# An expert layer's Strassen products: a list scheduler written in the kernel, sums kept in DRAM, and three products split once more

## The chip, the cores and the metric

The kernel runs on one core of one Trainium2 chip. The metric is the device time of one execution, in microseconds, as the median of several runs. Lower is better.

## The reference

Block-sparse attention (4 batches, 8 heads, 768 positions, head size 64) is followed by a mixture of 8 experts over its output `x` (3072 tokens of 512 features):

```
logits = x @ w_gate
P = exp(logits - logits.max())
for _ in range(8):
    P /= P.sum(1, keepdims=True) + 1e-09
    P /= P.sum(0, keepdims=True) + 1e-09
    P *= N / E
for e in range(8):
    h = maximum(x @ w1[e], 0)        # w1[e]: 512 x 1024
    out += P[:, e:e+1] * (h @ w2[e]) # w2[e]: 1024 x 512
```

Every expert sees every token, so the expert part is 8 times two large matrix products.

## The kernel before, in words

The attention comes first, in an order that is written out by hand: every step has a place in a table of time steps, and `in_order` chains the instructions of each engine to one another in that order. It leaves `x`, transposed, in DRAM (`xd`), for each batch as the seven operands that a Strassen-like scheme (Winograd's form) needs. Every operand is kept as two float16 halves, a high and a low one, so one product of float32 quality is three float16 matmuls: high by high, high by low, low by high.

The expert part runs 32 passes, `i = 4 e + b` for expert `e` and batch `b` (768 tokens). A pass has two stages:

- Stage one (`stage1`, L1199 on) computes `h` transposed: 1024 hidden features by 768 tokens, split in two by two quarters, so seven products instead of eight. Each product is 512 features by 384 tokens with 256 inner features and is made in four strips (`qi`) of 128 features. One strip of one product is one PSUM bank and 6 matmuls of 384 columns (2 chunks of 128 inner features, 3 float16 terms; L1208). DVE and ACT take each bank out at once: `comb` (L1220) adds it to what the earlier products gave. Then ReLU (ACT, in place), four sums or differences on GpSimd, and for each of the seven results a high half (ACT, L1230) and a low half (DVE L1234 or L1240, GpSimd L1240). These are the seven `h` operands of stage two.
- Stage two (`stage2`, L1333) makes seven products, each 384 tokens by 256 output features with 512 inner ones, in three strips (`ci`) of 128 tokens: one strip is one bank and 12 matmuls of 256 columns. The products 0, 5, 6 share a bank in turn (`FOLLOWS`), and 4, 2 another. DVE adds each bank, times the expert's weight of each token, to the sum of the outputs `acc` in SBUF (L1357; ACT writes the first ones, L1354).

All of `acc` (4 batches) stays in SBUF from the first expert to the last. PSUM has four banks for stage one (`ps_h`) and four for stage two (`ps_y`), each handed out in turn. The loop at the end interleaves strips of stage one of pass `i + 1` with products of stage two of pass `i`. The side work (reads, low halves, weight sums and splits, the balance iterations of P) is put into slots by `Slots`, which counts the planned load of each engine; the final order on each engine is then chosen by the framework's own scheduler, so an instruction of the expert part can also stand ahead of the attention's last ones.

The weights of one expert, 2 MB each for `w1` and `w2`, share one raw buffer. For each matrix ACT makes eight magnitude sums (L108), PE spreads their maximum over the partitions (L114), GpSimd forms the sums of quarters (L1087, L1094 for `h`), ACT and DVE split each of the seven operands (L1072, L1076). The `x` operands are loaded anew for each pass (L227, 7 x 384 KB).

Of the kernel before, what the change touches and what calls it, by code (L numbers as in the profile page):

```python
# [24 lines left out]
TOP = 2.0 ** 12  # L25
# [4 lines left out]
HDOWN = 2.0 ** -20  # L30
HUP = 2.0 ** 20
EPS = 1e-9
PORDER = (0, 1, 5, 6, 3, 4, 2)
NHT = 30
NU = 8
LOP = (2, 3)
LOPE = (2, 3, 5)
NLE = 99
LEADS, LAGS = (1.0, 1.0, 1.0), (1.0, 1.0, 1.0)
SD = (2, 3, 4, 5)  # L40
PRE, LB2, LB1 = 0, 1, 1
PIN = 0
TW = 100
TF = 146
HQ = 300
NHA = 10
LATE = 40
# [3 lines left out]
LAV = 3  # L51


@with_exitstack
def tile_sparse_attention_moe(
# [79 lines left out]
    def scale_power(tag, s, inv):  # L135
# [6 lines left out]
        nc.vector.tensor_scalar(s, s, TOP, None, ALU.mult)  # L142
        nc.vector.tensor_scalar(inv, a, 1.0 / TOP, None, ALU.mult)

# [35 lines left out]
    def scale_steps(which, e, vector=nc.vector, scalar=nc.scalar):  # L180
# [18 lines left out]
        def power():  # L199
            vector.tensor_reduce(out=a, in_=wr["all", which], axis=AX.X, op=ALU.max)  # L200
            vector.tensor_scalar(a, a, TINY, HUGE, ALU.max, ALU.min)
            ai = a.bitcast(I32)
            vector.tensor_scalar(ai, ai, 0x7F800000, None, ALU.bitwise_and)
            vector.reciprocal(s, a)
            vector.tensor_scalar(s, s, TOP, None, ALU.mult)
            vector.tensor_scalar(inv, a, 1.0 / TOP, None, ALU.mult)

# [138 lines left out]
    def finish_x(b):  # L346
        xf = xfs.pop(b).rearrange("p k c t -> p k (c t)")
        quad = {
            (j, k): xf[:, j * KH : (j + 1) * KH, k * TH : (k + 1) * TH]
            for j in range(2) for k in range(2)  # L350
        }

        def split(src, p, nm):
            st = xst.tile([P, 2, KH, TH], F16, tag="xs", name=f"xs_{b}_{nm}")
            nc.scalar.activation(st[:, 0], src, AF.Copy)
            nc.vector.tensor_tensor(out=st[:, 1], in0=src, in1=st[:, 0], op=ALU.subtract)
            if p is not None:
                nc.sync.dma_start(out=xd[b][:, p], in_=st)
            return st

        def plain(k):
            sts = [
                split(quad[j, k], {(0, 0): 0, (1, 0): 1, (1, 1): 2}.get((j, k)), f"b{j}{k}")
                for j in range(2)
            ]
            ps = bank[0](f"lg_{b}_{k}")
            for i in range(CH):
                for kc in range(KD):
                    for m, (l, w) in enumerate(((1, gh), (0, gl), (0, gh))):
                        nc.tensor.matmul(  # L370
                            ps[:, i * NE : (i + 1) * NE],
                            lhsT=sts[kc // KH][:, l, kc % KH, i * P : (i + 1) * P],
                            rhs=w[:, kc],
                            start=(kc == 0 and m == 0), stop=(kc == KD - 1 and m == 2),
                        )
            t0 = b * NC + k * CH
            nc.vector.tensor_scalar(
                lg[:, t0 : t0 + CH].rearrange("p t e -> p (t e)"), ps[:, : CH * NE],
                inv_v[:, b : b + 1], inv_g, ALU.mult, ALU.mult,
            )  # L380

        def diff(nm, x, y, out, p):
            nc.gpsimd.tensor_tensor(out=out, in0=x, in1=y, op=ALU.subtract)
            split(out, p, nm)

        x00, x01, x10, x11 = (quad[j, k] for j in range(2) for k in range(2))
        return [
            lambda: plain(0),
            lambda: plain(1),
            lambda: diff("t1", x01, x00, x00, 4),  # L390
            lambda: diff("t3", x11, x01, x01, 6),
            lambda: diff("t2", x11, x00, x00, 5),
            lambda: diff("t4", x10, x00, x10, 3),
        ]

    with ExitStack() as actx:
# [18 lines left out]
        plan = xfp.tile([P, 2, S], BF16, tag="xf", name="plan")  # L415
        onehot = plan[:, 0]
# [148 lines left out]
        def scale_v(b):  # L565
            sv[b] = small.tile([P, 1], F32, tag="sv", name=f"sv_{b}")
            scale_power(f"v{b}", sv[b], inv_v[:, b : b + 1])
# [246 lines left out]
        def split_gate():  # L814
            scale_power("g", sg, inv_g)
# [116 lines left out]
        xlast = finish_x(B - 1)  # L932

    class InOrder:
        def __init__(self, engine):
            self.engine = engine

        def __getattr__(self, name):
            call = getattr(self.engine, name)
            if not PIN:  # L940
                return call
            return lambda *a, **kw: tc.keep_in_program_order(call(*a, **kw))

    class Pinned:
        vector, scalar, gpsimd = (InOrder(x) for x in (nc.vector, nc.scalar, nc.gpsimd))
# [3 lines left out]
    )  # L949
    sk = mpool("sk", 1)  # L950
    upool = mpool("upool", NU)
    hA = mpool("hA", 1)
    hB = mpool("hB", 1)
    big = mpool("big", 1)
    def spare(n):
        return sk.tile([P, n], F32, name=f"spare_{next(count)}")

    count = iter(range(99))
    ps_h = mpool("ps_h", 4, space=PSUM)
    ps_y = mpool("ps_y", 4, space=PSUM)  # L960

    DH = DM // 2
    w2p = [big.tile([P, 2, KF // 2, DH], F16, name=f"w2p_{p}") for p in range(NP)]
    hfree = [
        (hA if n < NHA else hB).tile([P, 2, TH], F16, name=f"h_{n}") for n in range(NHT)
    ]
    accs = {b: big.tile([P, NC, DM], F32, name=f"acc_{b}") for b in range(B // 2)}
    bank[0] = lambda nm: ps_y.tile([P, 512], F32, tag="py", name=nm)
    spread_bank[0] = lambda nm: ps_h.tile([P, 512], F32, tag="ph", name=nm)

    def acc(t):
        return accs[t // NC][:, t % NC]

    def finish_late():
        slots.need(("late", 0, 0))
        late.close()
        right = mpool("right", 1, side="right")
        for b in range(B // 2, B):
            accs[b] = right.tile([P, NC, DM], F32, name=f"acc_{b}")

    aside = set()

    def not_earlier(fn):
        made = nc.cur_bb.bb.instructions
        n = len(made)
        fn()
        for ins in list(made[n:]):
            if ins.engine not in SIDE:
                continue
            for old in reversed(made[:n]):  # L990
                if old.engine == ins.engine and old.name not in aside:
                    tc.add_manual_dep(ins, old.name, behind, reason="not_ahead_of_its_place")
                    break
            aside.add(ins.name)

    class Slots:
        def __init__(self):
            self.now, self.pe, self.busy = 0, 0.0, [0.0, 0.0, 0.0]
            self.urgent, self.lazy = [], []
            self.last = 0  # L1000

        def add(self, fn, key, delay=1, lazy=False, dve=0.0, act=0.0, pool=0.0, gap=0):
            queue = self.lazy if lazy else self.urgent
            queue.append((fn, key, self.now + delay, (dve, act, pool), gap))

        def charge(self, costs):
            self.busy = [x + c for x, c in zip(self.busy, costs)]

        def run(self, queue, n):
            fn, key, _, costs, _ = queue.pop(n)  # L1010
            self.charge(costs)
            if queue is self.lazy:
                self.last = self.now
            if key[0] in ("scale", "w1", "w2"):
                not_earlier(fn)
            else:
                fn()

        def fits(self, costs):
            return all(  # L1020
                not c or x <= self.pe + lead
                for x, c, lead in zip(self.busy, costs, LEADS)
            )

        def tick(self, pe, dve, act=0.0):
            self.now += 1
            self.pe += pe
            self.busy = [max(x, self.pe - lag) for x, lag in zip(self.busy, LAGS)]
            self.charge((dve, act, 0.0))
            n, held = 0, set()  # L1030
            while n < len(self.urgent):
                _, key, ready, costs, _ = self.urgent[n]
                if key not in held and ready <= self.now and self.fits(costs):
                    self.run(self.urgent, n)
                    n, held = 0, set()
                    continue
                held.add(key)
                if key[0][0] == "sum":
# [358 lines left out]
    for i in range(NI):  # L1397
# [35 lines left out]
        if last:  # L1433
            parts[1]()
# [43 lines left out]
```

## Time and profile before

| what | value |
|---|---|
| median of 3 runs | 2236.8 us (2235.66 to 2239.47) |
| span of the profiled execution | 2232.8 us |
| PE busy | 2162.7 us (97%) |
| weight loads busy | 1596.3 us (71%) |
| DVE, POOL, ACT busy | 1671.7, 1412.6, 1285.1 us |
| first stage-one matmul | 414.07 us |
| DMA | 192.36 MB, 86 GB/s |

The page gives no time of the profiled execution other than its span; the time beside it is the median of the runs. PE is TensorE's matmuls, PEld its weight loads, DVE VectorE, ACT ScalarE, POOL GpSimd, SP the engine that issues most DMAs. Matmuls overlap, so the mean duration of one (as in a group's row) is longer than the distance at which they start. A wait is shown in square brackets, with the instruction that ended it.

### The profile page before, as it was taken

What the parts mean: (1) busy time and instruction counts of PE and PEld (TensorE: products, weight loads), DVE (VectorE), ACT (ScalarE), POOL (GpSimd) and SP (SyncE); (2) the same over time, 40 slices, a digit from 0 to 9 for tenths busy, and PEclk for the clock granted to TensorE, in tenths of its full rate; (3) what the DMA queues carried; (4) which work ended last, traced back from release to release, by engine and by line L of the source; (5) the groups of instructions that cost most, each with busy time, mean ns of one, the idle gap of its engine ahead of it and who ended that gap; (6) DMA issues with size and microseconds to landing.
All of it is one profiled execution on the core that took longest, in us unless ns stands there. A gap on an engine that the chain in (4) does not pass through costs nothing.

```text
span 2232.8 us, 47313 instructions
## 1 busy us (share of the span) xinstructions
PE 2162.7 (97%) x18892; PEld 1596.3 (71%) x18892; DVE 1671.7 (75%) x2927; ACT 1285.1 (58%) x2393; POOL 1412.6 (63%) x1481
## 2 busy tenths in 40 slices
PE   6999999889999999999999999999999999999999
PEld 4777766566777777777777777777677767776777
DVE  8888888778778767866786678667866786678664
ACT  5788888754566546554555455545554555455442
POOL 5556678685568555855685658565856585658553
PEclk9999999999999999999999999999999999999999
DMA  7766965312121212121212121212121212121221
GB/s 167 151 154 138 209 146 126 130 69 88 51 88 50 88 50 88 50 89 50 88 50 88 50 88 50 89 50 88 50 88 50 88 51 88 51 88 58 79 79 51
DMA packets 195347, 192.36 MB, mean 86 GB/s; under 512 B 132125, under 2 KB 150581, under 8 KB 195125
## 3 DMA queue, kind: packets, MB, share of 16 engines
q1 hardware_dynamic: 194560, 189.30, 29.3%
q8 instruction: 148, 2.42, 0.5%
q14 instruction: 75, 0.61, 0.1%
q10 hardware_dynamic: 564, 0.03, 0.0%
HBM read 140.54 MB, written 17.30 MB: 71 GB/s over the span
## 4 chain that ended last, share of the span: by engine, by line
PE 64%; DVE 11%; POOL 9%; ACT 7%; issue 4%; DMA 4%; DVEq 0%; SPq 0%; POOLq 0%; ACTq 0%
PE py L1333 26%; PE p L1208 25%; PE u L767 3%; DMA r<-in_moe_w_dram 3%; PE m L669 2%; PE m L672 2%; PE t L702 2%; PE t L705 2%; ACT h L1230 2%; POOL r L1087 2%; ACT unread L108 2%; POOL s L1282 2%; POOL h L1240 1%; DVE attic L1076 1%; POOL r L1094 1%
## 5 line engine op out<-in xcount | busy, mean ns | idle before, releaser
L1333 PE MATMUL py<-w2p,h 128*128 128x256 f16 x8064 | 952.4, 273 | 12.2 <-ACT acc L1354 4.2
L1333 PEld LDWEIGHTS <-h 128*128 128x128 f16 x8064 | 787.7, 98 | 154.0 <-issue 16.6
L1240 POOL TENSOR_TENSOR h<-u,h 128x384 f16<-128x384 f32 x128 | 124.4, 972 | 558.8 <-ACT h L1230 541.4
L1208 PEld LDWEIGHTS <-attic 128*128 128x128 f16 x3072 | 299.5, 98 | 202.2 <-issue 20.5
L1208 PE MATMUL p<-attic 128*128 128x384 f16 x2304 | 412.0, 326 | 12.7 <-DVE a L1220 8.0
L1208 PE MATMUL p<-arena 128*128 128x384 f16 x2304 | 415.3, 326 | 5.9 <-DVE u L1220 2.7
L1357 DVE SCALAR_TENSOR_TENSOR acc<-py,spare,acc 128x256 f32<-128x256 f32 (+1 forms) x588 | 295.0, 514 | 145.3 <-PE py L1333 143.2
L1208 PEld LDWEIGHTS <-arena 128*128 128x128 f16 x2304 | 225.2, 98 | 134.1 <-issue 7.8
L1230 ACT ACTIVATE h<-c 128x384 f16<-128x384 f32 x256 | 132.5, 520 | 319.9 <-DVE c L1220 263.0
L1220 DVE SCALAR_TENSOR_TENSOR a<-p,a 128x384 f32<-128x384 f32 x384 | 211.2, 550 | 22.7 <-PE p L1208 16.6
L678 DVE TENSOR_REDUCE top<-m 128x1 f32<-128x768 f32 x192 | 181.7, 951 | 46.7 <-PE m L672 45.8
L710 ACT ACTIVATE pe<-t,qk 128x768 int32<-128x768 f32 x192 | 172.3, 899 | 68.7 <-PE t L705 60.3
L1230 ACT ACTIVATE h<-s 128x384 f16<-128x384 f32 x128 | 66.8, 522 | 174.3 <-POOL s L1282 174.2
L1230 ACT ACTIVATE h<-r 128x384 f16<-128x384 f32 x256 | 131.3, 519 | 61.3 <-POOL r L1094 58.3
L1240 DVE TENSOR_TENSOR h<-s,h 128x384 f16<-128x384 f32 x128 | 106.2, 830 | 79.5 <-ACT h L1230 79.3
L1094 POOL TENSOR_TENSOR r<-s,r 128x384 f32<-128x384 f32 x128 | 153.6, 1200 | 10.0
L1094 POOL TENSOR_TENSOR c<-c,r 128x384 f32<-128x384 f32 x128 | 151.1, 1180 | 10.0
L1282 POOL TENSOR_TENSOR s<-a,u 128x384 f32<-128x384 f32 x128 | 140.9, 1101 | 17.3 <-ACT a L1279 17.1
L1208 PE MATMUL p<-arena,attic 128*128 128x384 f16 x768 | 146.2, 326 | 5.4 <-ACT a L1255 4.7
L1240 POOL TENSOR_TENSOR h<-r,h 128x384 f16<-128x384 f32 x128 | 133.9, 1046 | 18.3 <-ACT h L1230 15.2
L724 POOL TENSOR_SCALAR pl<-pe 128x768 f16<-128x768 uint16 x112 | 96.3, 864 | 70.9 <-ACT pe L710 68.8
L1087 POOL TENSOR_TENSOR r<-r 128x256 f32<-128x256 f32 (+1 forms) x106 | 119.0, 1148 | 31.0 <-DVE arena L1076 31.0
(206 smaller groups left out, 3717.3 us busy)
## 6 DMA issues: line engine op xcount, KB each, us to landing
arena<-xd SPq DMA_DIRECT2D x128, 384.0 KB, 3.9
attic<-xd SPq DMA_DIRECT2D x96, 384.0 KB, 4.2
r<-in_moe_w_dram SPq DMA_DIRECT2D x16, 2048.0 KB, 8.7
arena<-in_q_dram SPq DMA_DIRECT2D x16, 384.0 KB, 4.3
arena<-in_k_dram SPq DMA_DIRECT2D x16, 384.0 KB, 4.7
arena<-in_v_dram SPq DMA_DIRECT2D x4, 1536.0 KB, 7.8
xd<-xs_t SPq DMA_DIRECT2D x16, 384.0 KB, 2.9
out_dram<-acc SPq DMA_DIRECT2D x48, 128.0 KB, 1.7
```

The costliest lines, as they stand in the source:

```text
L678: nc.vector.tensor_reduce(out=tops[n][:, c : c + 1], in_=sc[:, :S], axis=AX.X, op=ALU.max)
L710: nc.scalar.activation(pe, sc[:, :S], AF.Exp, bias=EXP_SHIFT, scale=qk[n // 2][3])
L724: nc.gpsimd.tensor_scalar(lo, low, FINE, 1.0, ALU.mult, ALU.mult)
L1087: lambda c=c: Pinned.gpsimd.tensor_tensor(out=out[:, c], in0=x[:, c], in1=y[:, c], op=op),
L1094: nc.gpsimd.tensor_tensor(out=out, in0=x, in1=y, op=ALU.subtract)
L1208: nc.tensor.matmul(ps, lhsT=w1p[p][:, l, kc, fs], rhs=xp[p][:, r, kc], start=(kc == 0 and m == 0), stop=(kc == KH - 1 and m == 2),)
L1220: nc.vector.scalar_tensor_tensor(out=t, in0=ps, scalar=HDOWN, in1=other, op0=ALU.mult, op1=ALU.add)
L1230: nc.scalar.activation(h[:, 0], src, AF.Relu if relu else AF.Copy)
L1240: eng.tensor_tensor(out=h[:, 1], in0=src, in1=h[:, 0], op=ALU.subtract)
L1282: nc.gpsimd.tensor_tensor(out=s1, in0=a1, in1=u3, op=ALU.add)
L1333: nc.tensor.matmul(py, lhsT=hs[i, p, kc][:, l, tsl], rhs=w2p[p][:, r, kc], start=(old is None and kc == 0 and m == 0), stop=(kc == KF // 2 ...
L1357: nc.vector.scalar_tensor_tensor(out=dst, in0=src, scalar=c, in1=dst, op0=ALU.mult, op1=ALU.add)
```

## The change

The attention is unchanged, but for scale constants (`TOP1`, `HDOWN`, `HUP`). The expert part is written anew:

- Every step is a job with its engine or a choice of two (DVE or GpSimd), a planned duration, the jobs that it needs, and the buffers that it takes and drops. `Plan.run` is a list scheduler: it runs through planned time and starts on each engine, among the jobs that are ready, the one with the earliest deadline; on PE the one with the earliest planned place `pt`. Stage one and stage two are two streams with an order of their own. The order found is the program's: `in_order` chains all of it, on each engine, behind the attention's last instruction.
- In stage one a bank X takes the products 0, 5, 4, 2 one after another, without being cleared; after each the sum is read. So PE waits for a read before it goes on in the bank.
- From expert 1 on the products 6, 3 and 1 (`TWO`) of stage one are themselves made of seven products of quarters, for all strips at once: 21 groups of 6 matmuls of 192 columns instead of 12 groups of 6 of 384. Their operands are sums of quarters: of `w1` in SBUF (`sums`, on GpSimd for each expert, then split by ACT and DVE), of `x` prepared once in the first four passes (`prep_x`) and kept in DRAM (`xsd`), from where `xs` is loaded in each pass.
- `acc` is no longer kept in SBUF. Each pass loads two pieces of 768 KB, adds, and stores them (`accd`, in DRAM); three tiles are handed round.
- The output is stored in pieces of 384 KB.

The core of it:

```diff
-        a1 = fresh("a1")
-        nc.scalar.activation(a1, product(0), AF.Copy, scale=HDOWN)
-        tick(0, 1)
-        r11 = fresh("r11")
-        comb(r11, product(1), a1)
...
+    def run(self):
...
+                    if e == "PE":
+                        best = min(ok, key=lambda j: (j.pt is not None, j.pt if j.pt is not None else j.seq))
+                    else:
+                        for j in sorted(ok, key=lambda j: (j.dl, j.seq)):
...
+        def inner_group(p, r, bk, fresh):
...
+            def fn():
+                for c in range(2):
+                    for m, (l, rr) in enumerate(((0, 0), (0, 1), (1, 0))):
+                        nc.tensor.matmul(
+                            bk.tile[:, c * HT : (c + 1) * HT], lhsT=lhs(l, c), rhs=rhs(rr),
+                            start=(fresh and c == 0 and m == 0), stop=(m == 2),
+                            skip_group_check=True,
+                        )
...
+        def inner_product(p, addend=None):
...
+            j0, e0 = go(0, X, True, deps)
+            ta, ca = spot(X, 0, 0, j0, e0)
+            j1, e1 = go(1, Z, True, ())
...
+            j6, e6 = go(6, Y, True, ())
+            tc_, cc = spot(Y, 1, 1, j6, e6)
+            j5, e5 = go(5, X, False, (ca,))
+            tb, cb = spot(X, 1, 0, j5, e5)
+            j3, e3 = go(3, Y, False, (cc,))
...
+            j4, e4 = go(4, X, False, (cb,))
...
+            j2, e2 = go(2, X, False, (wrote[1, 1],))
...
+        if two:
+            got[6] = inner_product(6)
+            got[3] = inner_product(3, got[6])
+            got[1] = inner_product(1)
...
+            if two:
+                for q, (j, end) in outer(0, X, True, {}).items():
+                    r_[q] = scaled_add(cell(R, q), bank(X[q]), cell(R, q), [j] + rdep, dl=end + SLK)
+                for q, (j, end) in outer(5, X, False, {q: (r_[q],) for q in qis}).items():
+                    c_[q] = scaled_add(cell(C, q), bank(X[q]), cell(C, q), [j] + cdep, dl=end + SLK)
+                for q, (j, end) in outer(4, X, False, {q: (c_[q],) for q in qis}).items():
+                    u_[q] = scaled_add(cell(U, q), bank(X[q]), cell(U, q), [j] + udep, dl=end + SLK)
...
+                for q, (j, end) in outer(0, X, True, {}).items():
+                    k0[q] = scaled_copy(cell(R, q), bank(X[q]), (j,), take=first(R, q), dl=end + SLK)
+                for q, (j, end) in outer(1, Z, True, {}).items():
+                    r_[q] = scaled_add(cell(R, q), bank(Z[q]), cell(R, q), (j, k0[q]), drop=(Z[q],), dl=end + SLK)
...
+        pieces = [hold("acc") for _ in range(2)]
+        loaded = {}
+        if e:
+            for j in range(2):
+                ld = plan.dma(
+                    lambda j=j: nc.sync.dma_start(out=pieces[j].tile, in_=accd[b][j]), 768,
+                    (accstore[i - B, j],), take=(pieces[j],),
+                )
...
+        if e < NE - 1:
+            for j in range(2):
+                accstore[i, j] = plan.dma(
+                    lambda j=j: nc.sync.dma_start(out=accd[b][j], in_=pieces[j].tile), 768,
+                    tuple(writes[j]), drop=(pieces[j],),
+                )
...
+    S1A = NP * NF * 0.978
+    S1B = len(TWO) * 7 * 0.497 + (NP - len(TWO)) * NF * 0.978
+    S2 = NP * CH * 1.312
...
+        stage2(i, clock + SHIFT, length)
...
+            stage1(i + 1, clock, length)
+        clock += length
+    plan.run()
+    for fn in plan.order():
+        in_order(fn)
```

## Rows read from the trace of the kernel before

**Rows 1.** The page's busy line: us, share of the span, instructions.

```profile
PE 2162.7 (97%) x18892; PEld 1596.3 (71%) x18892; DVE 1671.7 (75%) x2927; ACT 1285.1 (58%) x2393; POOL 1412.6 (63%) x1481
```

**Rows 2.** Busy time by stretch: length, then engines, granted clock, DMA share, GB/s.

```profile
414.00:500.00 86.00, 75.16 (x535) 50.43 (x532) 66.42 (x106) 55.45 (x117) 63.28 (x60) 1.00 0.19 66
500.00:650.00 150.00, 144.18 (x1162) 107.48 (x1161) 118.98 (x233) 80.09 (x166) 87.41 (x80) 1.00 0.22 77
700.00:2229.00 1529.00, 1507.04 (x11521) 1124.99 (x11518) 1105.07 (x1959) 792.73 (x1593) 957.35 (x907) 1.00 0.20 69
```

**Rows 3.** Groups by line and form, PE: busy us, mean ns, idle before.

```profile
L1333 PE MATMUL py<-w2p,h 128*128 128x256 f16 x8064 | 952.4, 273 | 12.2 <-ACT acc L1354 4.2 <-DVE acc L1357 3.5 <-ACT w2p L1072 1.4
L1208 PE MATMUL p<-arena 128*128 128x384 f16 x2304 | 415.3, 326 | 5.9 <-DVE u L1220 2.7 <-DVE a L1220 1.8 <-DVE c L1220 0.9
```

**Rows 4.** Timeline of PE, undisturbed groups: start, length, instructions merged.

```profile
609.97 3.09 PE L1208 MATMUL p<-arena 128*128 128x384 f16 x18
612.90 1.14 PE L1208 MATMUL p<-arena,attic 128*128 128x384 f16 x6
...
621.05 2.78 PE L1333 MATMUL py<-w2p,h 128*128 128x256 f16 x24
623.67 0.33 PE L1208 MATMUL p<-arena 128*128 128x384 f16 x1
```

**Rows 5.** Timeline of PE, first and last of 45 short matmuls.

```profile
412.72 0.19 PE L767 MATMUL u<-vq,pl 128*128 128x66 f16 x1
...
414.04 0.19 PE L767 MATMUL u<-vh,pe 128*128 128x66 f16 x1
```

**Rows 6.** Groups by line and form, weight loads of those matmuls.

```profile
L767 PEld LDWEIGHTS <-pe 128*128 128x128 f16 x2304 | 118.4, 97 | 5.9 <-issue 0.8
```

**Rows 7.** Timeline of PE, ACT, DVE, where the attention ends.

```profile
414.07 3.09 PE L1208 MATMUL p<-arena 128*128 128x384 f16 x18
...
424.97 0.27 PE L114 MATMUL u<-ident,ma_w 128*128 128x128 f32 x1
...
433.69 0.49 PE L798 MATMUL u<-ident,xn 128*128 128x128 f32 x3
...
416.93 0.63 ACT L108 ACTIVATE unread<-r 128x512 bf16<-128x512 f32 x1 [3.06 <-DMA r<-in_moe_w_dram]
...
423.86 0.15 DVE L194 TENSOR_REDUCE ma_w<-mx_w 128x1 f32<-128x8 f32 x1
```

**Rows 8.** Groups by line and form, side engines.

```profile
L1220 DVE SCALAR_TENSOR_TENSOR a<-p,a 128x384 f32<-128x384 f32 x384 | 211.2, 550 | 22.7 <-PE p L1208 16.6
L1255 ACT ACTIVATE a<-p 128x384 f32<-128x384 f32 x128 | 61.4, 480 | 45.1 <-PE p L1208 44.2
L1279 ACT ACTIVATE a<-a 128x384 f32<-128x384 f32 x128 | 66.3, 518 | 3.5 <-DVE a L1220 2.6
L1087 POOL TENSOR_TENSOR r<-r 128x256 f32<-128x256 f32 x64 | 62.4, 1002 | 0.0
L1072 ACT ACTIVATE w2p<-r,sw 128x1024 f16<-128x1024 f32 x48 | 54.4, 1136 | 15.2 <-POOL r L1087 15.2
L1076 DVE SCALAR_TENSOR_TENSOR w2p<-r,sw,w2p 128x1024 f16<-128x1024 f32 x48 | 66.1, 1378 | 12.9 <-ACT w2p L1072 12.9
```

**Rows 9.** Timeline of DVE and PE, a wait of PE for an add.

```profile
1386.48 0.54 DVE L1220 SCALAR_TENSOR_TENSOR a<-p,a 128x384 f32<-128x384 f32 x1
...
1387.08 1.14 PE L1208 MATMUL p<-attic 128*128 128x384 f16 x6 [1.34 <-DVE a L1220]
```

**Rows 10.** The page's DMA issues: count, KB each, median us to landing.

```profile
attic<-xd SPq DMA_DIRECT2D x96, 384.0 KB, 4.2
r<-in_moe_w_dram SPq DMA_DIRECT2D x16, 2048.0 KB, 8.7
...
out_dram<-acc SPq DMA_DIRECT2D x48, 128.0 KB, 1.7
xd<-xs_b SPq DMA_DIRECT2D x12, 384.0 KB, 3.0
```

More of the change, by code (lines that the diff above doesn't have):

```diff
@@ L344, in plan_x @@
             at(T + 3, FIRST, x_store, b, nm, p)
[L346 to L394, printed above, removed]
     with ExitStack() as actx:
@@ L931, in tile_sparse_attention_moe @@
                 in_order(fn, *a)
[L932 to L945, printed above, removed]
     mpool = lambda name, bufs, **kw: ctx.enter_context(
@@ L981, in tile_sparse_attention_moe @@
[L981 to L1038, printed above, removed]
-                    held.update((("h", key[1], p),) + key[1:] for p in (2, 4, 5, 6))
-                n += 1
-            while self.lazy and self.due(self.lazy[0]):
-                self.run(self.lazy, 0)
-        def due(self, item):
-            _, _, ready, costs, gap = item
-            return max(ready, self.last + gap) <= self.now and self.fits(costs)
-        def settle(self, i, qi):
-            while any(x[1][1:] <= (i, qi) for x in self.urgent):
-                self.run(self.urgent, 0)
-        def need(self, key):
-            for queue in (self.urgent, self.lazy):
-                while any(x[1] == key or x[1][0] == key for x in queue):
-                    self.run(queue, 0)
@@ L1057, in tile_sparse_attention_moe @@
-    ET = mybir.EngineType
-    SIDE = (ET.DVE, ET.Activation, ET.Pool, ET.PE)
-    slots = Slots()
-    def scale_w(which, e):
-        parts, whole, spread, power = scale_steps(which, e, Pinned.vector, Pinned.scalar)
-        key = ("scale", which, e)
-        for k, part in enumerate(parts):
-            slots.add(part, key, 8 if k == 0 else 1, True, act=0.65)
-        slots.add(whole, key, 1, True, dve=0.1)
-        slots.add(spread, key, 1, True, gap=5)
-        slots.add(power, key, 1, True, dve=0.8, gap=2)
@@ new lines, in tile_sparse_attention_moe, with v3, seq @@
+    accd = [
+        [dram.tile([P, CH, DM], F32, name=f"accd_{b}_{j}") for j in range(2)] for b in range(B)
+    ]
+    xsd = [dram.tile([P, NP, 2, 4, TH // 2], F16, name=f"xsd_{b}") for b in range(B)]
+    sums = {}
+    shelf["xs"] = [xst.tile([P, 2, KH, TH], F16, tag="xs", name=f"stage_{n}") for n in range(4)]
+    plan = Plan(shelf)
+    job, hold = plan.job, plan.hold
+    def v3(t):
+        return t.rearrange("p (c t) -> p c t", c=2)
+    def seq(steps, deps=(), **kw):
+        last = tuple(deps)
+        for eng, dur, fn in steps:
+            last = (job({eng: dur}, fn, last, **kw),)
+        return last[0]
@@ L1139, in first, with split @@
[L1139 to L1143 removed]
+        stored = {}
+        def split(src, p, deps):
+            st = hold("xs")
+            hi = job({"ACT": 0.83}, lambda: nc.scalar.activation(st.tile[:, 0], src, AF.Copy), deps, take=(st,))
+            lo = job(
+                {"DVE": 1.3},
+                lambda: nc.vector.tensor_tensor(out=st.tile[:, 1], in0=src, in1=st.tile[:, 0], op=ALU.subtract),
+                (hi,),
+            )
+            if p is not None:
+                stored[p] = plan.dma(
+                    lambda: nc.sync.dma_start(out=xd[b][:, p], in_=st.tile), 384, (lo,), drop=(st,)
+                )
+            return st, lo
@@ new lines, in tile_sparse_attention_moe, with raw_load, scale_jobs, make @@
+    scaled, split_done, used1, used2 = {}, {}, {}, {}
+    last_s3 = [()]
+    raw_free = [()]
+    pwe = {}
+    def raw_load(which, e):
+        return plan.dma(lambda: load_w(which, e), 2048, raw_free[0])
+    def scale_jobs(which, e, loaded):
+        cell = {}
+        def make():
+            cell["steps"] = scale_steps(which, e)
+        parts = []
+        last = job({"-": 0.0}, make, (loaded,))
+        for k in range(8):
+            last = job({"ACT": 0.81}, lambda k=k: cell["steps"][0][k](), (last,))
+            parts.append(last)
+        whole = job({"DVE": 0.16}, lambda: cell["steps"][1](), parts)
+        bk = hold("s1", ordered=False)
+        def spread():
+            spread_bank[0] = lambda nm: bk.tile
+            cell["steps"][2]()
+        pe = job({"PE": 0.3}, spread, (whole,), take=(bk,))
+        power = job({"DVE": 1.2}, lambda: cell["steps"][3](), (pe,), drop=(bk,), rush=True)
+        scaled[which, e] = power
+        return parts, power
```

1228 lines of the change are left out of this document (873 added, 355 removed).

## The prediction

> **What bounds the kernel now.** I read the page's busy line first: TensorE (PE) is busy 2162.7 of 2232.8 us, 97%, far above DVE, POOL and ACT [rows 1]. That is an average, so the second view is the busy time by stretch. Of the 1529 us from 700 to 2229 us PE is busy 1507.0, so 22.0 are idle (1.4%), with DVE at 72%, POOL at 63% and ACT at 52%; the expert part's start is worse: 10.8 us idle of 86 (414 to 500 us) and 5.8 of 150 (500 to 650 us) [rows 2]. The clock is granted in full throughout. So in the expert part, which is four fifths of the span, the time is the number of columns that PE streams, plus some 39 us of gaps.
>
> The third view gives the price of a column. Busy means overlap (273 and 326 ns a matmul [rows 3]), so I take the distance of starts: eighteen 384-column matmuls run from 609.97 to 612.90, 162.8 ns each; twenty-four 256-column ones from 621.05 to 623.67, 109.2 ns each [rows 4]. The line through both is 0.419 ns a column plus 2 ns. A 192-column matmul, which the kernel before does not have, should then take 82.4 ns (estimate from these rows).
>
> **The change part by part.**
>
> *Quarter products.* A pass (one expert, one batch) has 7 products x 4 quarters x 6 = 168 stage-one matmuls of 384 columns and 252 stage-two ones of 256. From expert 1 on, in 28 passes, three products (72 matmuls, 72 x 0.1628 = 11.72 us) become 3 x 7 x 6 = 126 matmuls of 192 columns: 126 x 0.0824 = 10.38 us. Saved: 1.34 us a pass; I take 1.3, so 28 x 1.3 = 36 us. From one side the bound is plain column count (72 x 384 against 126 x 192, an eighth of 11.72 us, 41 us in all), from the other a weight load that paces the short matmul. There are 54 more weight loads a pass. A load row says 97 ns [rows 6], more than 82; but 45 matmuls of 66 columns, each with a load of its own, start between 412.72 and 414.07, every 30 ns [rows 5]. Loads overlap each other and the matmuls, so they don't pace 82 ns. The Trainium skill speaks against this ("TensorE: Matmul & The Clock Gate", section on LDWEIGHTS): it prices a load at columns/1.2 ns, 107 ns for 128 columns, and if that were a rate the edit would lose; rows 5 disagree with it as a rate. It is rival A.
>
> *What the quarter products add beside PE.* In each pass DVE makes 25 scaled adds where it made 28 (0.55 us each), ACT makes 12 copies out of PSUM for 4 (0.48 us), and one ReLU a quarter is now part of such a copy (4 fewer at about 0.5 us); per expert come 12 POOL sums of 256 columns (1.0 us), 3 ACT (1.14 us) and 3 DVE weight splits (1.38 us) [rows 8]. A pass of some 54 us gets ACT + 3.8 - 2.1 + 0.9 = +2.6 us (52% becomes 57%), POOL + 3.0 us (63% becomes 69%), DVE - 1.7 + 1.0 = -0.6 us. Nothing comes near PE's share, so I cost all of it at nothing; if that cover failed on POOL, the 3 us a pass would be 84 us. The sums of x in the first four passes (12 rounds of five element-wise steps and a split on DVE or POOL, a load and a store of 384 KB) lie in expert 0, where DVE now makes 12 scaled adds a pass and not 28 (8.8 us less a pass): nothing.
>
> *PSUM chains.* Products 0, 5, 4, 2 add up in one bank, each read between. This takes adds from DVE but makes PE wait for the reader before it may go on in that bank. No such wait stands in the trace; its parts do. A matmul's record ends about 0.16 us after its slot (326 against 163 ns) [rows 3, 4], the hand-over took 0.06 us (DVE's add ended at 1387.02, PE went on at 1387.08) [rows 9], the read 0.55 us: 0.16 + 0.06 + 0.55 + 0.06 = 0.83 us. It is hidden where other groups (0.98 us, or 1.31 us of stage two) stand in between. The outer chain always has two products' groups or the other quarter's between, so nothing; the inner chains are rival B.
>
> *Fixed order.* All expert instructions are now chained behind the attention's on each engine. Before, the framework put stage one ahead of the attention's last work: first at 414.07, while PE still owed the w2 spread (424.97) and the last turns (433.69) [rows 7]. In the new order PE stops after the attention's values (about 415), the w2 magnitudes start on ACT at 416.93 when the load lands, eight at about 0.74 us end at 422.9, then DVE's maximum, the spread and six transposes: stage one starts at about 424. PE loses 9 us (bounds: 0, and the 19.6 us to 433.7). Behind it stage one of pass 0 runs with fewer DVE reads and without being ranked against attention work, so of the 16.6 us idle from 414 to 650 us [rows 2] I leave 7: 9.6 back (bounds: 16 back, 10 lost). Of the steady 22.0 us I leave 18: the longest single waits are for a DVE add that stood behind a weight split (1.34 us at 1387.08 [rows 9]), and the products 6, 3 and 1 that now open a pass have their weights free a pass's half earlier: 4 back. Bounds: all 22 back; as much again lost, since an order fixed from planned durations can't move up when one step is late.
>
> *Output sums in DRAM.* Each pass loads and stores two pieces of 768 KB and loads 3 x 384 KB more. Landing of such a load lies between 4.2 (384 KB) and 8.7 us (2048 KB) [rows 10]; I take 5.5. With a third tile the next piece is asked for some 20 us ahead, and DMA has a 0.20 share in the steady stretch [rows 2]; twice to three times the bytes leave it under 0.6. Nothing, if the order on SP holds: each load stands behind the waits of everything issued before it. Rival C is that cover failing.
>
> *End.* The last output goes as 384 KB, not 128: a store of 384 KB took 3.0 us against 1.7 [rows 10], +1.3 us. New scale constants: nothing.
>
> Sum on the profiled span: 2232.8 - 36 + 9 - 9.6 - 4 + 1.3 = 2193.5 us. The runs' median, 2236.8, is 4.0 above that execution's span; the page gives no other time of it. So the forecast is 2197.5 us, 1.8% less, with an own range of 2180 to 2216 (steady gaps 8 to 30 us, start 5 either way).
>
> **Rivals.**
>
> A, weight loads pace the quarter matmuls. If a load really held PE for its 97 ns [rows 6], 126 x 0.097 = 12.2 us would stand where 11.7 stood: +0.5 us a pass, +14 instead of -36, and the time is 2197.5 + 50 = 2247 us. Only the load's record speaks for it, rows 5 speak against. By the page's 107 ns it would be 13.5 us a pass and some 2283 us.
>
> B, the bank round trip, on the slower side. In an inner product the groups go 0, 1, 6, 5, 3, 4, 2 over three banks, each 0.49 us. Run with nothing between, group 3 waits 0.83 - 0.49 = 0.34 us for the reader of 6, and group 2 the whole 0.83 us for the reader of 4: 1.2 us a product, nearly three times the 0.43 us that a product saves. A stage-two group in each gap (1.31 us) hides both. It decides from 33 of the 84 inner products on (39.3 us of gain / 1.2); at 60 it costs 72 us: 2270 us. For it: the order is fixed, so a late reader on DVE delays every chain behind it, and DVE's share is the highest of the side engines. Against: stage two has 21 groups a pass to put between 21 inner groups, and the DVE, ACT and POOL durations are steady.
>
> C, the gain is eaten: late pieces of the sums or late x loads (SP's queue in order) hold the first reads of each stage two by some 1.3 us: 28 x 1.3 = 36 us, 2234 us, no change. For it: SP's issues double; against: the DMA share above.
>
> D, the gaps go: a plan with deadlines takes the remaining 18 + 7 us of idle nearly all away: 2197.5 - 25 = 2172 us. For it: side engines at 52 to 72% leave room. Against: semaphore hand-overs at fixed places.
>
> **How the numbers follow.** Forecast 0.64, D 0.14, C 0.07, B 0.11, A 0.04. The forecast and D are faster, C is split (0.03 faster, 0.04 same), A and B are slower: 0.81, 0.04, 0.15, where 0.2% (4.5 us) is what a measurement of this kernel can tell from no change. The range 2168 to 2240 holds the forecast, C and most of D (0.83); what it leaves out is A, B and the best of D. The likeliest case alone has 2180 to 2216.
>
> **What would show it.** Quarter matmuls of 192 columns should start every 82 ns (every 97 or more: A). PE's idle from 700 us on should be near 18 us (over 55: B, and then the waits of PE's stage-one line name DVE or ACT reads of the inner products). The first stage-one matmul should come at about 424 us with a gap of some 9 us before it. Waits of DVE's stage-two line for the DMA of the sums would mean C. DVE, ACT and POOL should stay under 80%. The prediction is wrong if PE's busy time in the expert part does not fall by about 36 us, or if what falls comes back as PE waits.

## The result and the profile after

The changed kernel took 2201.2 us (median of 4 runs, 2200.0 to 2204.3) against 2238.1 in the same set of runs: ratio 0.9837, 95% interval 0.9823 to 0.9851. The forecast was 2197.5, so the number came out within 0.2%. Where it came from did not: the experiments below show that the quarter products, which carry nearly the whole gain in the forecast's sum, brought back in waits what they saved in columns, and that the rest of the change, above all the planned order, which stands there at about nothing, is worth some 40 us without them.

The profiled execution took 2204.3 us with a span of 2202.5. Its busy line, which answers [rows 1]:

```profile
PE 2131.7 (97%) x20404; PEld 1699.5 (77%) x20404; DVE 1740.9 (79%) x2835; ACT 1357.3 (62%) x2570; POOL 1575.0 (72%) x1602
```

PE is as full as before, with DVE and POOL closer behind it. By stretch, as in [rows 2] (length, busy time of PE, PEld, DVE, ACT, POOL, granted clock, DMA share, GB/s):

```profile
414.00:500.00 86.00, 76.00 (x674) 51.96 (x671) 62.81 (x84) 64.97 (x133) 59.04 (x52) 0.94 0.36 119
500.00:650.00 150.00, 136.81 (x1013) 100.92 (x1012) 139.26 (x210) 88.43 (x187) 103.52 (x91) 0.97 0.46 149
700.00:2199.00 1499.00, 1489.03 (x13158) 1235.15 (x13155) 1161.01 (x1915) 859.16 (x1756) 1113.56 (x1031) 1.00 0.44 146
```

Steady idle went from 22.0 to 10.0 us. In the stretch from 500 to 650 us it grew from 5.8 to 13.2, DVE is 93% busy there, and PE's granted clock was at its lower level for part of it (0.97 on average). The quarter matmuls themselves (timeline of PE):

```profile
1033.84 0.66 PE L1575 MATMUL p<-arena,attic 128*128 128x192 f16 x6
1034.34 0.66 PE L1575 MATMUL p<-xs,sums 128*128 128x192 f16 x6
1034.83 1.47 PE L1866 MATMUL y<-w2p,h 128*128 128x256 f16 x12
```

Twelve of them take 0.99 us, 82.5 ns each, where the forecast had 82.4 [rows 4]. The hand-over from the attention, beside [rows 7]:

```profile
423.89 0.63 ACT L329 ACTIVATE unread<-r 128x512 bf16<-128x512 f32 x1 [2.66 <-DMA r<-in_moe_w_dram]
...
429.93 0.16 DVE L415 TENSOR_REDUCE ma_w<-mx_w 128x1 f32<-128x8 f32 x1 [6.32 <-ACT unread L329]
...
430.15 0.48 PE L335 MATMUL u<-ident,ma_w 128*128 128x128 f32 x1 [7.55 <-DVE ma_w L415]
...
433.19 3.09 PE L1546 MATMUL p<-arena 128*128 128x384 f16 x10
```

PE waits 7.55 us for the maximum of w2, where the forecast had a gap of some 9, and stage one starts at 433.19 instead of 414.07. Part of that is not the change: in this execution the attention, whose instructions are the same, was 7.8 us later by its end (its last value product starts at 422.41; in before it starts at 418.00, with 3.4 us of stage one ahead of it). Over 5 us of that came in one place, where PE waited for a transposing DMA and the clock then fell (row of the wait, and that stretch of after; before has PE busy for all 30 us there, at 1.00):

```profile
272.42 0.58 PE L877 MATMUL t<-qt,kt 98*128 98x512 f16 x1 [2.32 <-DMA qt<-qs]
```

```profile
260.00:290.00 30.00, 27.68 (x368) 19.53 (x364) 21.63 (x35) 21.07 (x34) 13.87 (x22) 0.89 0.81 171
```

The other kernels' executions show this wait or not, whatever the edit, so below medians are compared, and stretches that lie behind the attention. Two such stretches of before and of after serve as the measure (same columns), first of before:

```profile
500.00:700.00 200.00, 192.68 (x1525) 143.05 (x1524) 153.93 (x303) 114.88 (x243) 123.69 (x118) 1.00 0.24 82
700.00:2150.00 1450.00, 1428.74 (x10888) 1063.09 (x10886) 1058.27 (x1873) 767.08 (x1542) 924.75 (x875) 1.00 0.21 70
```

Then of after:

```profile
500.00:700.00 200.00, 182.79 (x1400) 139.01 (x1399) 176.48 (x285) 117.01 (x247) 136.38 (x124) 0.96 0.46 151
700.00:2150.00 1450.00, 1440.58 (x12743) 1194.54 (x12741) 1129.03 (x1863) 844.35 (x1725) 1088.95 (x1009) 1.00 0.45 149
```

Idle of PE in the two: 7.3 and 21.3 us before, 17.2 and 9.4 after. What PE waits for between 500 and 700 us of after (us in all, times, longest; L1250 is the balance iterations of P):

```profile
PE p L1250 <- DVE spare L1244: 6.2, 3, 3.5
PE p L1575 <- ACT u L1528: 4.0, 1, 4.0
PE p L1546 <- DVE pair L1519: 3.5, 1, 3.5
PE y L1866 <- DVE acc L1902: 2.8, 1, 2.8
PE p L1250 <- DVE pair L1519: 0.8, 1, 0.8
```

Idle time leaves out what a lower clock costs and what the overlapping records of matmuls hide. So PE's lost time was also worked out from the starts of all matmuls in the traces: the distance from each start to the next, less the slot that a matmul of its size takes undisturbed (82.5, 109.2 and 162.5 ns for 192, 256 and 384 columns, the few other sizes likewise). From the attention's last value product to the last matmul, PE lost 55 us in before and 54 in after: against before, the change took columns away and left the lost time as it was.

### The profile page after: what moved, and what is told of

It reads as the page before. It is cut to its first block, busy times and chain, and to the rows that moved or that the text cites. A ratio compares the mean times of both kernels' runs of the same rounds, so it can differ in the third digit from the quotient of the medians.

```text
span 2202.5 us, 50394 instructions
## 1 busy us (share of the span) xinstructions
PE 2131.7 (97%) x20404; PEld 1699.5 (77%) x20404; DVE 1740.9 (79%) x2835; ACT 1357.3 (62%) x2570; POOL 1575.0 (72%) x1602
## 4 chain that ended last, share of the span: by engine, by line
PE 75%; DVE 9%; POOL 9%; issue 3%; ACT 2%; DMA 2%; SPq 0%; DVEq 0%; POOLq 0%; ACTq 0%
PE y L1866 31%; PE p L1546 19%; PE p L1575 12%; POOL r L1299 4%; PE u L939 4%; POOL u L1784 3%; PE t L877 2%; PE m L841 2%; PE m L844 2%; PE t L874 2%; DVE h L1752 2%; POOL h L1750 1%; DVE top L850 1%; DMA qt<-qs 1%; DVE stage L1491 1%
## 5 line engine op out<-in xcount | busy, mean ns | idle before, releaser
L1866 PE MATMUL y<-w2p,h 128*128 128x256 f16 x8064 | 973.9, 273 | 2.9 <-DVE acc L1902 2.8
L1750 POOL TENSOR_TENSOR h<-pair,h 128x384 f16<-128x384 f32 x294 | 306.0, 1053 | 278.7 <-ACT h L1761 262.8
L1902 DVE SCALAR_TENSOR_TENSOR acc<-y,spare,acc 128x256 f32<-128x256 f32 (+1 forms) x588 | 302.4, 517 | 170.9 <-PE y L1866 168.1
L1761 ACT ACTIVATE h<-pair 128x384 f16<-128x384 f32 x640 | 321.0, 518 | 137.1 <-POOL pair L1784 66.1
L1784 POOL TENSOR_TENSOR u<-u,pair 128x384 f32<-128x384 f32 x256 | 306.0, 1211 | 64.7 <-ACT u L1528 47.9
L1519 DVE SCALAR_TENSOR_TENSOR pair<-p,pair 128x384 f32<-128x384 f32 x384 | 212.4, 555 | 137.7 <-PE p L1546 136.0
L1746 ACT ACTIVATE pair<-pair 128x384 f32<-128x384 f32 x384 | 194.2, 516 | 102.6 <-DVE pair L1519 93.0
L1752 DVE SCALAR_TENSOR_TENSOR h<-pair,h 128x384 f16<-128x384 f32 x218 | 198.4, 924 | 9.5 <-ACT h L1761 9.4
L1575 PEld LDWEIGHTS <-sums 128*128 128x128 f16 x2016 | 174.6, 98 | 18.8 <-issue 14.0
L1575 PE MATMUL p<-xs,sums 128*128 128x192 f16 x1512 | 161.8, 247 | 10.1 <-ACT u L1528 7.6
```

Source lines behind the costliest of these rows:

```text
L1519: lambda: nc.vector.scalar_tensor_tensor(out=out_(), in0=bank_(), scalar=HDOWN, in1=add(), op0=ALU.mult, op1=ALU.add),
L1575: nc.tensor.matmul(bk.tile[:, c * HT : (c + 1) * HT], lhsT=lhs(l, c), rhs=rhs(rr), start=(fresh and c == 0 and m == 0), stop=(m == 2), ski ...
L1746: return job({"ACT": 0.52}, lambda: nc.scalar.activation(view(), view(), AF.Relu), dep)
L1750: nc.gpsimd.tensor_tensor(out=out_, in0=x, in1=y, op=ALU.subtract)
L1752: nc.vector.scalar_tensor_tensor(out=out_, in0=x, scalar=1.0, in1=y, op0=ALU.mult, op1=ALU.subtract)
L1761: lambda: nc.scalar.activation(h.tile[:, 0], src(), AF.Relu if relu else AF.Copy),
```

## The experiments

Each was timed against the kernel before (2236 to 2238 us in the sets of runs); "idle" is that of PE in 500 to 700 and 700 to 2150 us of the profiled execution.

| kernel | us | ratio (95%) | idle, us |
|---|---|---|---|
| before | 2237 | 1 | 7.3, 21.3 |
| after | 2201.2 | 0.9837 (0.9823 to 0.9851) | 17.2, 9.4 |
| e1, whole products | 2197.3 | 0.9821 (0.9806 to 0.9835) | 0.3, 0.0 |
| e3, w2 in the plan | 2198.6 | 0.9825 (0.9809 to 0.9842) | 18.1, 14.6 |
| e5, measured durations | 2187.4 | 0.9776 (0.9761 to 0.9792) | 16.3, 2.6 |
| e8, e5 + spread sums | 2192.6 | 0.9798 (0.9784 to 0.9813) | 14.6, 9.9 |
| e9, e3 + e5 + e8 | 2181.9 | 0.9745 (0.9729 to 0.9761) | 16.7, 6.9 |
| e14, e9 + merged sums | 2180.2 | 0.9741 (0.9724 to 0.9759) | 18.7, 3.1 |
| e13, e1 + e3 + durations | 2186.0 | 0.9765 (0.9746 to 0.9785) | 0.5, 0.0 |
| e12, e9 without sums of x | 2174.8 | 0.9717 (0.9701 to 0.9734) | 5.3, 12.2 |
| e7, inner products bare | 2411.9 | 1.0782 (1.0760 to 1.0803) | 20.7, 151.6 |
| e11, order not fixed | 2345.0 | 1.0480 (1.0457 to 1.0502) | 18.0, 96.7 |
| e4, twice the sums' traffic | 2304.5 | 1.0299 (1.0284 to 1.0314) | 20.8, 79.9 |
| e4b, e4 + a faster plan | 2206.2 | 0.9858 (0.9830 to 0.9886) | 13.2, 20.3 |

One thing limits what small differences in this table tell. Every edit makes the plan deal the whole order anew: e3 touches only the hand-over, and the steady idle went from 9.4 to 14.6 us; e8 sets deadlines in the first four passes only, and it went from 2.6 to 9.9. Some 5 to 7 us of steady idle between two plans with quarter products can so be the luck of the order, and not the edit.

**The quarter products undone (e1).**

```diff
-TWO = (6, 3, 1)
+TWO = ()
```

> The changed kernel with the three products left whole in all passes (no quarter products, and so no sums of x and w1 quarters). Theory (columns): PE streams 28 x 1.29 = 36 us more, and the sums of x leave DVE and POOL in the first four passes, which gives back some 10 to 15 of the gap between 500 and 660 us: about 2201 + 36 - 13 = 2224 us. Rival (the list order made the gain, the quarter products little): 2205 us or less. Rival (weight loads pace the quarter matmuls after all, so they save nothing): 2190 us, without the sums' gap.

It took 2197.3 us, and the forecast's own theory fell. All columns are back, and the time is no longer (the intervals overlap, so that it is shorter is not shown). Its stretches say why:

```profile
500.00:700.00 200.00, 199.74 (x1537) 149.91 (x1535) 149.96 (x265) 131.46 (x278) 124.99 (x114) 1.00 0.33 110
700.00:2150.00 1450.00, 1450.00 (x11115) 1087.72 (x11114) 977.69 (x1542) 850.19 (x1780) 916.36 (x835) 1.00 0.37 125
```

PE has no gap left at all from 700 to 2150 us. All that is left of the change (the planned order, the PSUM chains, the sums in DRAM) is thus worth 40 us by itself. The quarter products then save their 36 us of columns and bring back 17 + 9 us of recorded idle, some 8 us by the clock (0.96 of 200 us), and the rest as shorter losses that the records hide. Worked out from the starts of the matmuls, as above, PE lost 15 us in e1 behind the attention (13.5 of it up to 500 us, the hand-over), against 54 in after and 55 in before: 39 us more by the quarter products, 40 less by everything else. Which share of the 40 the order has, and which the chains, which take additions from DVE, no run tells: e1 with the framework's order was not tried.

**The order not fixed (e11).**

```diff
     for fn in plan.order():
-        in_order(fn)
+        fn()
```

> The changed kernel with the same steps written in the same order, but without the chain that fixes them on each engine: the framework's own scheduler orders the expert part, as in the kernel before. Theory (the fixed order of a plan is what took the steady idle from 22 to 10 us, and costs the hand-over): the first stage-one matmul comes ahead of the attention's last ones again (some 10 us earlier), steady idle from 700 us on rises above 25 us: 2205 to 2260 us. Rival (the order of writing and the PSUM chains do it, not the fixing): 2195 us or less.

2345 us, slower than the kernel before by 5%: the same steps, written in the same order but ordered by the framework, cost PE these waits most:

```profile
PE p L1575 <- ACT u L1528: 35.5, 35, 3.2
PE y L1866 <- DVE acc L1902: 24.2, 17, 2.8
```

So with quarter products the steps need the fixed order: without it the steady idle is 96.7 us, with it 9.4. One part of the expectation failed: the first stage-one matmul still came only at 431.26, behind the same wait for w2,

```profile
428.23 0.47 PE L335 MATMUL u<-ident,ma_w 128*128 128x128 f32 x1 [7.64 <-DVE ma_w L415]
```

so the fixing is not what holds the hand-over; whether it is the banks, taken over from the attention, was not tried.

**The bank round trip (e7).**

```diff
+                    if e == "PE" and tight:
+                        mine = [j for j in mine if j.stream != "2"]
```

(`tight` holds from an inner product's first group to its last.)

> The scheduler may not put a stage-two group between the seven groups of an inner product, so each runs bare in its three banks. Theory (bank round trip, hidden in the changed kernel by the stage-two groups): each of the 84 inner products waits 0.34 us before group 3 and 0.83 us before group 2, 1.2 us in all, 84 x 1.2 = 100 us: about 2300 us, with PE's waits on the quarter-product line for DVE and ACT near 100 us. Rival (reads are fast enough without cover): under 2220 us.

2412 us, 211 more than the changed kernel: rival B's mechanism is real. Where nothing else is late the waits are 0.30 and 0.65 us a product, somewhat under the 0.34 and 0.83 worked out [rows 4, 9]; in all, the loss is twice the 100 us expected (timeline of PE, then its waits: us in all, times, longest):

```profile
1413.12 0.66 PE L1581 MATMUL p<-xs,attic 128*128 128x192 f16 x6 [0.30 <-DVE u L1624]
...
1414.92 0.66 PE L1581 MATMUL p<-attic,sums 128*128 128x192 f16 x6 [0.65 <-DVE pair L1662]
```

```profile
PE p L1581 <- ACT u L1534: 83.1, 23, 9.3
PE p L1581 <- DVE pair L1662: 75.7, 84, 2.3
```

The 84 waits for `pair` are one for each inner product, 0.9 us on average; 83 us more are 23 waits for copies by ACT, up to 9.3 us, which the pricing did not have. The cover in the changed kernel is nearly complete: its quarter-product line waits 12.7 us in all.

**The traffic of the sums (e4, e4b).**

```diff
+                ld = plan.dma(
+                    lambda j=j: nc.sync.dma_start(out=pieces[j].tile, in_=accd[b][j]), 768,
+                    (ld,),
                 )
...
+                pieces[j].also(plan.dma(
+                    lambda j=j: nc.sync.dma_start(out=acce[b][j], in_=pieces[j].tile), 768,
+                    (accstore[i, j],),
+                ))
```

> The changed kernel with each piece of the output sums loaded twice, one load after the other, and stored a second time to another place in DRAM: 86 MB more. Theory (the DRAM traffic of the sums is hidden: DMA share 0.45, the piece is asked for early): 2201 us, within 0.3%. Rival (late pieces hold stage two): 28 passes x 1.3 us or more, 2237 us and up, with DVE's stage-two line waiting for DMA.

2304.5 us, far beyond even the rival, but DVE waited for no DMA of the sums. The plan's own transfer rate was the suspect, so e4b changed that alone, 190 to 380 GB/s:

```diff
-    DMA_RATE, DMA_LAND = 190.0, 2.0
+    DMA_RATE, DMA_LAND = 380.0, 2.0
```

> As e4 (twice the traffic of the output sums, 2304 us), but the plan reckons with 380 GB/s for its transfers in place of 190. In e4 the plan itself thought the transfers too slow for PE (about 11 MB a pass by 190 GB/s is 58 us, a pass of PE 54), so it laid the order round a bound that the chip (DMA share 0.55) did not show. Theory (the order cost it, not the transfers): below 2220 us. Rival (the transfers themselves are late): 2260 us or more, with DVE's stage-two line or PE's stage-one lines waiting for DMA.

2206 us. The stretch from 700 us of e4 and then of e4b:

```profile
700.00:2150.00 1450.00, 1370.13 (x11834) 1118.20 (x11833) 1116.34 (x1812) 801.26 (x1638) 955.74 (x890) 0.99 0.55 195
```

```profile
700.00:2150.00 1450.00, 1429.67 (x12601) 1183.92 (x12599) 1128.78 (x1845) 829.71 (x1697) 1078.13 (x989) 1.00 0.59 203
```

The same bytes at a higher rate and 60 us less idle: the 98 us between e4 and e4b were an order laid round a bound that existed only in the plan. Rival C is out: in after no engine waits for a piece of the sums. Doubled, the traffic is nearly hidden: behind 700 us of e4b ACT waits six times for a piece, 10.9 us in all, and ACT and POOL 43 us for weights, while the time is 5 us above after's, inside the intervals. The changed kernel at 380 GB/s without the added traffic was not run, so what the higher rate gives by itself is open.

**Durations of the plan (e5).** What DVE's steps really took in the changed kernel (minimum, median and maximum of each line):

```profile
L1752 DVE SCALAR_TENSOR_TENSOR h<-u,h x149: 541/954/2110, 455.5 to 2171.9; 128x384 f16<-128x384 f32 x149
...
L1491 DVE TENSOR_TENSOR stage<-stage x32: 296/1035/1405, 537.8 to 644.5; 128x192 f32<-128x192 f32 x32
...
L1519 DVE SCALAR_TENSOR_TENSOR pair<-p,pair x384: 541/558/560, 437.7 to 2162.5; 128x384 f32<-128x384 f32 x192
```

The plan had 0.65 and 0.36 us for the first two, near their minima. The steps with both inputs in SBUF take up to four times that; the addition with an input in PSUM, in the last row, hardly varies.

```diff
-                    {"DVE": 0.36, "POOL": 0.75},
+                    {"DVE": 0.87, "POOL": 0.71},
...
-                        {"DVE": 0.65, "POOL": 1.02},
+                        {"DVE": 0.92, "POOL": 1.05},
```

> Only the planned durations of five kinds of steps are set to what the changed kernel's trace shows (quarter sums of x on DVE 0.87 for 0.36, on POOL 0.71; sum of halves 1.2 and 2.3; low halves 0.92 and 1.05 for 0.65 and 1.02, of the ReLU kind 0.75; POOL sums 1.2 for 1.12). Theory (the first passes are held by DVE, which got work because the plan thought it short): DVE falls below 90% between 500 and 660 us, PE's idle there falls from about 20 us to 8 or less, steady idle stays near 10: 2189 us. Rival (the idle there is the chain of the balance iterations and the fixed order, whatever the durations): 2198 to 2204 us.

2187.4 us, as expected, though by another road: the steady idle, which was to stay, fell from 9.4 to 2.6 us, that of the first passes hardly (17.2 to 16.3). With the scatter between plans, what the durations themselves are worth of the 14 us is not shown. What stands in the first passes (timelines of DVE and PE in e5):

```profile
624.55 4.23 DVE L1491 TENSOR_TENSOR stage<-stage 128x192 f32<-128x192 f32 x4
...
629.17 0.41 DVE L1902 SCALAR_TENSOR_TENSOR acc<-y,acc 128x256 f32<-128x256 f32 x1
...
629.63 5.98 PE L1866 MATMUL y<-w2p,h 128*128 128x256 f16 x32 [6.68 <-DVE acc L1902]
```

Sums of x, bunched on DVE just before they are due, hold a read of stage two (L1902), and PE waits 6.7 us.

**The sums of x (e8, e14, e12).** e8 gives them deadlines spread over the four passes:

```diff
-                384, (lo,), drop=(st,),
+                384, (lo,), drop=(st,), dl=due,
```

> The kernel with the measured durations (2187 us), and with deadlines that spread the twelve sums of x evenly over the first four passes; before they had none of their own and ran one after another on DVE just ahead of the last moment (608 to 640 us, DVE 98% busy, PE idle for 6.7 and 5.7 us there and at half clock for 17 us). Theory (bunched sums of x on DVE hold the reads of stage two): PE's idle between 500 and 700 us falls from 24 us to 6 or less, no half clock there: 2187 - 20 - 5 = 2162 us. Rival (DVE has too much to do in the first passes wherever it stands): the idle only moves ahead, 2180 us or more.

A miss: 2192.6 us, no better than e5. Idle of the first passes fell by 1.7 us only (16.3 recorded in e5; the expectation's 24 fits only with the clock's loss counted in), and the steady idle rose by 7. e14 makes 36 steps of 48, on top of e9 (below):

> The kernel of e9 with two of the four quarter sums of x made by one instruction of twice the length (36 steps for 48). Theory (DVE and POOL are full in the first four passes, 92 and 97% between 500 and 660 us): some 10 us of their work go, half of it shows, 2177 us. Rival (the length of the chain, not the work): no change, 2182 us.

2180.2 against 2181.9 us, inside the intervals, so it tells nothing. e12 has no sums of x at all:

> The kernel of e9 (2182 us), leaving out the twelve sums of x and their split: what is loaded is stored as it is, so the quarter products get wrong operands of the same size. Theory (the sums of x in the first four passes are what costs the quarter products their gain): PE's idle between 500 and 750 us, 31 us in e9, falls to 8 or less, and 2182 - 23 = 2159 us. Rival (the idle comes from expert 0's own work, or from the first weights' quarter sums): 2175 us or more.

2174.8 us, 7 less than e9: the rival's number, not the theory's 2159. Idle in the first passes fell by 11.4 us, to 5.3, where the kernels with sums have 13 to 21, but 5.3 us more came in the steady part:

```profile
500.00:700.00 200.00, 194.74 (x1607) 154.84 (x1605) 155.13 (x270) 127.72 (x263) 153.60 (x139) 0.99 0.49 169
700.00:2150.00 1450.00, 1437.85 (x12673) 1191.09 (x12670) 1071.89 (x1778) 834.89 (x1713) 1101.18 (x1069) 1.00 0.43 147
```

So the sums are one cause of the first passes' gaps, not all that the quarter products cost.

**The hand-over (e3, e9, e13).** The w2 magnitudes, spread and power leave the attention's table and become jobs:

```diff
-            for n, part in enumerate(parts):
-                at(NTILE + n // 4, LATER, part)
-            at(NTILE + 2, LATER, whole)
-            at(NTILE + 2, LAST, spread)
-            at(NTILE + 3, LATER, power)
...
-            start = job({"-": 0.0}, views, (loaded,))
-            parts = [start]
-            scaled[2, e] = start
+            start = job({"-": 1.0}, views, (loaded,))
+            parts, _ = scale_jobs(2, e, start)
```

> The w2 magnitudes, their spread and the power move from the attention's end into the list scheduler's part, so the turns of the last x tile on PE no longer stand behind them. Theory (hand-over): the wait of PE of 7.6 us for the maximum goes, and with it the 10.2 us at half clock that follow it: the first stage-one matmul comes some 6 us earlier against the attention's end and the kernel takes about 2201 - 10 = 2191 us. Rival (stage one of pass 0 is held by the same side work wherever it stands, or stage two of pass 0 now waits for its weights): 2198 us or more.

2198.6 us: the rival's number. The wait for w2 is gone, and the first stage-one matmul starts 2.8 us behind the attention's last value product, not 10.8, but 5 us more idle came in the steady part. With whole products, where nothing takes it back, the same edit does count:

> Whole products in all passes, as in e1, with the w2 magnitudes in the plan and the measured durations of low halves and POOL sums. If the hand-over's loss is one of its own, it takes 2197 - 10 = 2187 us, and the quarter products are worth about 5 us beside it (e9: 2182). If the steady idle, 0.6 us in e1, comes back with the longer durations: above 2195 us.

2186.0 us against 2197.3 of e1. Its durations are changed too, but PE's idle is 0.5 and 0.0 us in the two stretches, as in e1, and the start is what moved: stage one begins 3.1 us behind the last value product, in e1 10.8. e9 adds the hand-over's edit to e5 and e8:

> Measured durations, spread sums of x, and the w2 magnitudes moved into the plan. If the hand-over step and the sums of x are two separate losses, the two gains add: 2162 - 10 = 2152 us. If the hand-over's gain is given back in the first passes, as when it was made alone (2198.6 against 2201), about 2160 us.

2181.9 us: less than the sum of the parts, and better than e13 by 4 us only, with intervals that overlap. Beside each other, e13 and e14:

```profile
500.00:700.00 200.00, 199.54 (x1564) 149.88 (x1562) 145.62 (x250) 133.64 (x279) 150.89 (x136) 1.00 0.33 110
700.00:2150.00 1450.00, 1450.00 (x11115) 1087.69 (x11114) 828.47 (x1352) 847.42 (x1781) 1071.50 (x1027) 1.00 0.37 125
```

```profile
500.00:700.00 200.00, 181.34 (x1436) 140.23 (x1435) 179.75 (x278) 122.98 (x255) 170.56 (x142) 0.97 0.48 161
700.00:2150.00 1450.00, 1446.94 (x12801) 1201.40 (x12800) 1102.06 (x1818) 847.38 (x1732) 1105.04 (x1071) 1.00 0.43 148
```

e14 is the fastest kernel that computes the whole layer (e12 does not), faster than before and after; e13, without any quarter product, is within 6 us of it, with intervals that overlap. So no gain by the quarter products is shown in a complete kernel; only e12, without the sums of x, lies clear of e13, by 11 us.

## Why the prediction was right, and where it was not

The time, the sign and the range held. By its own steps:

- *Quarter products, 36 us of columns*: right. 82.5 ns a matmul, 3528 of them for 2016 of 384 columns at 162.5 ns: 36.5 us, and PE's busy time in the expert part (from 414 us of before, from 422.6 of after) fell from 1774.9 to 1739.5 us. Rival A is out: a pair of a load and a matmul starts every 82.5 ns. The Trainium skill's price of a load ("TensorE: Matmul & The Clock Gate", section on LDWEIGHTS), by estimate 107 ns for 128 columns, is thus not the pace of such pairs in this trace.
- *What they add beside PE, "nothing"*: the step that failed. The forecast compared shares of busy time (DVE below 80% on average) and took mean durations as steady ones. The place to look was the first four passes, where DVE is 88% busy between 500 and 700 us and sums of x come in runs of 3 to 4 us ahead of reads that PE waits for. All but one of PE's waits in that stretch are for DVE; 7.0 of the 17 us stand before the balance iterations of P (L1250), which have nothing to do with the quarter products but share DVE with their sums. e1 has 0.3 us of idle in the whole stretch. e12 shows the part that the sums have, and e1 that there is more. In the steady part the sizes were off too: by the counts of stage-two matmuls (252 a pass), a pass between 700 and 2150 us has 1.2 us more on DVE than before (forecast -0.6), 4.9 more on POOL (+3.0) and 1.9 more on ACT (+2.6). By e1 the forecast's own last sign of being wrong is met: what fell came back as waits.
- *Fixed order*: mis-sized throughout. Steady: 4 us back forecast, 12 measured, 21 without quarter products (e1), and e11 shows that it needs the fixing. Start: 9.6 of 16.6 us back forecast; behind the first stage-one matmul after has 14.4 us idle up to 650 us, 1.2 of them before 500, so what came back there the first passes took again (5.8 before, 13.2 after); e1 has 1.4 in all. Hand-over: 9 us forecast; about 11 measured (19.1 later, less the 7.8 of the attention), with 10.2 us at the lower clock that the step had left out, and e11 shows that the chain on the engines is not its cause, as the step had it.
- *PSUM chains, rival B*: the undisturbed waits were priced a little too high (1.2 us a product, 0.95 measured), and the cover by stage two holds; e7 shows that its loss would cost twice what was reckoned.
- *Output sums in DRAM*: nothing, as forecast; a piece lands in 5.3 us (5.5 taken), and no engine waits for one.
- *End, +1.3*: not seen; from the last matmul's start to the end it is 4.3 us, 4.8 before.

So two errors, the gain of the order and the chains left out (some 35 us beyond the 4.6 in the sum) and the quarter products' cost left out (39 us), cancelled. That the sum came out so close is luck: one experiment (e1) tells the two apart, and the total alone never could.

## What to carry to other kernels

Where PE is full and a change takes columns away, ask first whether the gaps could be had instead: here a rewrite with a planned order closed 40 us of them without a column less, and the columns taken away then had to compete for side engines that, in the first passes, were nearly as full as PE. A planner's constants are part of the kernel: in e4 a transfer rate that was too low cost 98 us, and other durations changed the time by 14 (e5). And a change of many parts is known only when its parts have been run without each other.

## What the runs showed of the hardware

- In after, DVE's low halves (L1752, both inputs in SBUF) took 0.54 to 2.17 us for the same 384 columns, and the sums of 192 columns (L1491) 0.30 to 1.41, while the additions with an input in PSUM (L1519) stayed at 0.54 to 0.56, beside GpSimd operations too. The Trainium skill has a rule for this ("SBUF — State Buffer", section on who interferes with whom): a DVE instruction with two SBUF inputs contends with a GpSimd one that reads SBUF, for a shared port, and one with at most one SBUF input, outside the modes that use two ports, does not. The trace agrees: the 33 low halves with no GpSimd operation beside them took 0.54 to 0.56 us, the minimum of their line, against a median of 0.94 over all 367.
- The clock fell in the wake of short gaps: a stretch with waits of PE of 3.5, 2.8 and 4.0 us had 0.88 and then 0.85 granted (625 to 650 and 650 to 675 us of after, levels 1.2 and 2.4 GHz), while from 700 us on, where PE's longest wait was 1.4 us, after had 1.00. So, as an estimate, the gaps of the first passes (17.2 us) cost about half as much again (8 us, 0.04 of 200).
